# A recurrence and an FFN on one core: 66 elementwise instructions go from VectorE's queue to GpSimd's

## The chip, the core and the metric

The kernel runs as one program on one core of a Trainium2 chip. The metric is the device time of one execution in microseconds (us); the median of three runs stands for a kernel. A core has five engines with a queue of instructions each: TensorE (PE in the profile; its weight loads are PEld), VectorE (DVE), ScalarE (ACT), GpSimd (POOL) and SyncE (SP), which issues the DMAs here. Each engine takes its own instructions strictly in the order of the program; between engines only semaphores order things.

## The reference, cut to what matters

```python
# for each batch and head, over chunks of 32 steps, state is 16 x 32
L = exp(cum[:, None] - cum[None, :]) * causal           # decay inside a chunk
y = ((C @ B.T) * L) @ x  +  (C @ state) * exp(cum)      # within, and from the state
state = exp(sum(la)) * state + sum_j(B_j x_j decay_from_j)
# then all heads side by side make 256 values per token, 3072 tokens
h = x @ w_in                  # 256 -> 2048
out = softplus(h) @ w_out     # 2048 -> 256
```

## The kernel before

**Units.** The 4 x 768 tokens are cut into 24 units of 128 tokens (6 per batch). A unit's work is: `rm`, the table of decays inside the chunk (GpSimd cuts it out of `fc` with an affine select, function `decays`); `bp`, the scaled B (`scale_b`, VectorE); `sp`, the scores (TensorE); `m = sp * rm` (`weigh`, VectorE), which is the last reader of `rm`, whose buffer is then free for the unit two later; `zp`, the product of `bp` and x that updates the state (`update_some`, TensorE, for two units at a time: `zp18` is for units 18 and 19); `yp`, the unit's output (TensorE); and `yy = yp * gg` (`grow_pair`, VectorE).

**Two-part numbers.** The FFN multiplies in a format that keeps too few bits, so each operand is held as a high part and a low part (`xh` and `xl`, `wih` and `wil`, `gh` and `gl`, `woh` and `wol`) and a product is three matmuls: high by high, high by low, low by high. ScalarE makes a high part with a cast, and the low part is what is left (value minus high part). The low part of x is `xl`, two stretches of 256 tokens to a tile of 512; from unit 8 on (tile 2) it is made in the third stage of `grow_pair`.

**Tiles.** The FFN has 6 tiles of 512 tokens. For tiles 0 to 3 it goes plainly: `hp` (first product, 16 blocks `k`), ScalarE's softplus `e`, its parts `gh` and `gl`, and `acc` (second product). Tiles 4 and 5 are done together in eight rounds `p`, by a scheme that needs seven products in place of eight (`seven`), into `late_a` to `late_d`. It takes sums and differences of blocks of weights, made per round in `sums_of_weights`: first `both_w` (one instruction of 512 columns), four instructions `sums_w` of 128 columns, ScalarE's cast into `sw` (high), and one subtract of 512 columns into `sw` (low). Round `p`'s `late_b` is the first product that reads its `sw`. Round 0's sums are made among the units 20 to 23; those of round p + 1 are called, a stage at a time, during round p.

**The order.** Nothing is left to a scheduler: every instruction is marked to keep the program's order, and that order is written out by hand as a text of words, one word for one step (`Y14` is a stage of `grow_pair(14)`, `M16` of `weigh(16)`, `d18` is `decays(18)`, `B18` is `scale_b(18)`, `N18` is `update_some(18)`, `F3.0` is the first product of tile 3, block 0, `sw0` a stage of the sums of round 0). A piece of it, from the place that matters most below:

```python
P2.12 Y14 P2.11 P2.12 Y12 v18 N16 Z2.8 P2.11 v19 d18 F2.13 P2.13 S16 d19 gg18 M16 P2.13 S17 M17 Y14 Z2.9 M16
M17 F2.15 F2.14 B19 B18 v20 P2.12 P2.14 Q19 P2.14 Q18 P2.14 Z2.10 v21 Z2.11 P2.15 N18 N18 F3.0 P2.13 P2.15 C17
```

Buffers matter in one way: the tiles `both_w`, `sums_w`, `again` and `b_rows` take turns in two buffers (tag `w`), and six buffers hold the units' inputs `un`. `V` and `Pl` are VectorE and GpSimd, `A` is ScalarE; `WHOLE` is 12.

Of the kernel before, what the change touches and what calls it, by code (L numbers as in the profile page):

```python
# [10 lines left out]
F32 = mybir.dt.float32  # L11
# [6 lines left out]
ALU = mybir.AluOpType  # L18
PSUM = bass.MemoryType.PSUM

P = 128
# [11 lines left out]
WHOLE = 12  # L33
# [90 lines left out]
def recurrence_then_ffn(ctx: ExitStack, tc: tile.TileContext, un, late, at, al, w_in, w_out, const, outT):  # L124
# [24 lines left out]
    V, A, Pl, PE = (InOrder(e) for e in (nc.vector, nc.scalar, nc.gpsimd, nc.tensor))  # L149
# [12 lines left out]
    wih = cp.tile([P, 2, DFF], F32R, name="wih")  # L162
    wil = cp.tile([P, 2, DFF], F32R, name="wil")
# [247 lines left out]
    def x_parts(t0):  # L411
        j = max(i for i in range(len(sizes)) if starts[i] <= t0)
        if j not in xparts:
            xparts[j] = [p3.tile([P, 2, 512], F32R, tag=f"x{v}", name=f"x{v}_{j}", bufs=3) for v in "hl"]
        return xparts[j], t0 - starts[j]
# [24 lines left out]
    def scale_b(i):  # L440
        b, u = divmod(i, NU)
        if u < NU - 1:
            bp = mid[i]["bp"] = p2.tile([P, NH, N], F32, tag="bp", name=f"bp{i}", bufs=4)
            V.tensor_tensor(
                bp,
                un_s[i][:, U_B:U_C].rearrange("p (h n) -> p h n", n=N),
                f_tok[b][0][:, u, :].unsqueeze(2).broadcast_to([P, NH, N]),
                op=ALU.mult,
            )
# [184 lines left out]
    def grow_pair(i):  # L634
        y = p2.tile([P, 2, 2 * P], F32, tag="yy", name=f"yy{i}")
        if i >= 4 * (PAIRED + 1):
            ys[i % 4 * P] = y
        for g in range(2):
            V.tensor_tensor(y[:, g], mid[i]["yp"][g], gg_s[i, 2][:, g], op=ALU.mult)
        yield  # L640
        (xh, xl), c0 = x_parts(i * P)
        hi = xh[:, :, c0 : c0 + 2 * P]
        A.copy(hi, y)
        yield
        V.tensor_tensor(xl[:, :, c0 : c0 + 2 * P], y, hi.bitcast(F32), op=ALU.subtract)

    def update_some(i):
        some = [v for v in range(2) if i + v < NB * NU and (i + v) % NU < NU - 1]
# [179 lines left out]
    def sums_of_weights(p):  # L828

        def apart_of(w):  # L830
            return w.bitcast(F32).rearrange("p c (h k f) -> p c h k f", h=2, f=P)[:, :, :, p]

        t = p2.tile([P, 2, 2, P], F32, tag="w", name=f"both_w{p}")
        s = p2.tile([P, 4, P], F32, tag="w", name=f"sums_w{p}")
        both = sums_w[p] = p3.tile([P, 2, 4, P], F32R, tag="wraw", name=f"sw{p}", bufs=WRAW)
        V.tensor_tensor(t, apart_of(wih), apart_of(wil), op=ALU.add)
        yield
        V.tensor_tensor(s[:, 0], t[:, 0, 1], t[:, 1, 1], op=ALU.add)
        V.tensor_tensor(s[:, 1], s[:, 0], t[:, 0, 0], op=ALU.subtract)
        yield  # L840
        V.tensor_tensor(s[:, 2], t[:, 0, 0], t[:, 0, 1], op=ALU.subtract)
        V.tensor_tensor(s[:, 3], t[:, 1, 0], s[:, 1], op=ALU.subtract)
        A.copy(both[:, 0], s)
        yield
        V.tensor_tensor(both[:, 1], s, both[:, 0].bitcast(F32), op=ALU.subtract)

    def values_again():
        xh, xl = x_parts(starts[PAIRED])[0]
# [119 lines left out]
    def staged(f):  # L968
# [7 lines left out]
        return step  # L976

    sums_of_weights = staged(sums_of_weights)
    acts = {
        "warm": warm,  # L980
# [21 lines left out]
        "W": staged(split_stages),  # L1002
        "D": staged(lambda i: decays(i, 4 if i < 2 else 2)),
        "B": scale_b,
        "C": scale_c,
        "S": score,
# [13 lines left out]
        "J": within_some,  # L1020
        "N": staged(update_some),
        "Y": staged(grow_pair),
        "L": finish,
        "d": lambda i: whole(decays(i)),
        "Q": split_unit,
        "sw": sums_of_weights,
        "xa": values_again,
        "xs": staged(sums_of_values),
# [28 lines left out]
    for p in range(HALF):  # L1057
# [11 lines left out]
        if p < HALF - 1:  # L1069
            sums_of_weights(p + 1)  # L1070
# [83 lines left out]
```

## Time and profile before

| | |
|---|---|
| three runs | 317.13, 319.83, 319.46 us; median 319.46 us |
| profiled execution, from its first to its last instruction | 315.5 us |
| median less that span | 4.0 us |
| TensorE's granted clock, mean of the span | 0.999 |
| busy: PE, DVE, ACT, POOL | 309.6, 233.4, 194.5, 37.8 us |

The page does not give the time of the profiled execution itself, only its span. The span is what the engines' rows fill, and a run's time is 1.6 to 4.3 us longer than it by the three runs. "Busy" of an engine is the time in which at least one of its instructions runs.

### The profile page before, as it was taken

How to read it: one execution, taken by the hardware profiler on the slowest of the kernel's cores; microseconds unless marked ns; L12 is line 12 of the kernel's file. 1: busy time of each engine (PE TensorE's matmuls, PEld its weight loads, DVE VectorE, ACT ScalarE, POOL GpSimd, SP SyncE). 2: the span in 40 equal slices, each digit the busy share in tenths (PEclk: the TensorE clock that was granted, in tenths of full speed). 3: DMA queues.
4: the chain of work that ended last, by engine and by line, in shares of the span. 5: the costliest groups of instructions: out<-in, count | busy, mean ns of one | idle time of the engine just before them, and what ended most of it. 6: DMA issues, size and time to landing. Idle time of an engine off the chain costs nothing.

```text
span 315.5 us, 5504 instructions
## 1 busy us (share of the span) xinstructions
PE 309.6 (98%) x2081; PEld 246.8 (78%) x2081; DVE 233.4 (74%) x501; ACT 194.5 (62%) x367; POOL 37.8 (12%) x52
## 2 busy tenths in 40 slices
PE   8899999999999999999999999999999999999995
PEld 5557778878778778888887877888888888888884
DVE  4987876957547664789898989948478877877753
ACT  4999977877574244667667445326646567554761
POOL 3452010000003330012303303000000000000000
PEclk9999999999999999999999999999999999999999
DMA  6986075525000430262256022000001000000003
GB/s 209 334 269 229 2 249 179 183 94 163 1 0 3 132 137 0 82 219 66 69 179 208 0 96 92 0 2 1 0 2 66 0 0 2 0 0 2 2 0 133
DMA packets 15323, 26.87 MB, mean 85 GB/s; under 512 B 1472, under 2 KB 6208, under 8 KB 15296
## 3 DMA queue, kind: packets, MB, share of 16 engines
q1 hardware_dynamic: 15296, 26.52, 25.3%
q8 instruction: 16, 0.26, 0.3%
q14 instruction: 11, 0.09, 0.1%
HBM read 22.97 MB, written 3.54 MB: 84 GB/s over the span
## 4 chain that ended last, share of the span: by engine, by line
PE 92%; DMA 3%; SPq 2%; ACT 1%; issue 0%; DVE 0%; DVEq 0%; ACTq 0%
PE hp L146 28%; PE acc L146 28%; PE late_acc L146 13%; PE yp L146 5%; PE late_a L146 4%; PE late_d L146 3%; PE late_c L146 3%; PE sp L146 3%; SPq L155 2%; PE late_b L146 2%; DMA gg<-gd 2%; DMA head_in<-in_un 2%; PE zp L146 1%; PE fp L146 0%; ACT fc L146 0%
## 5 line engine op out<-in xcount | busy, mean ns | idle before, releaser
L146 DVE TENSOR_TENSOR gl<-e,gh 128x512 fp32r<-128x512 f32 x96 | 68.3, 720 | 26.3 <-ACT gh L146 26.2
L146 ACT CAST gh<-e 128x512 fp32r<-128x512 f32 x96 | 59.0, 619 | 25.2 <-PE acc L146 22.3
L146 ACT ACTIVATE e<-hp 128x512 f32<-128x512 f32 x64 | 37.3, 593 | 28.1 <-PE hp L146 28.0
L146 POOL TENSOR_SCALAR_AFFINE_SELECT rm<-fc 128x512 f32<-128x512 f32 (+2 forms) x40 | 34.6, 891 | 154.2 <-DVE m L146 141.4
L146 PE MATMUL hp<-xh,wih 128*128 128x512 f32 (+1 forms) x136 | 52.5, 386 | 0.0
L146 PE MATMUL hp<-xl,wih 128*128 128x512 f32 (+1 forms) x136 | 51.4, 378 | 0.0
L146 PE MATMUL hp<-xh,wil 128*128 128x512 f32 (+1 forms) x136 | 51.2, 377 | 0.0
L146 PE MATMUL acc<-gh,woh 128*128 128x512 f32 x128 | 50.7, 396 | 0.0
L146 PE MATMUL acc<-gl,woh 128*128 128x512 f32 x128 | 49.9, 390 | 0.0
L146 PE MATMUL acc<-gh,wol 128*128 128x512 f32 x128 | 49.9, 389 | 0.0
L146 DVE TENSOR_TENSOR m<-sp,rm 128x256 f32<-128x256 f32 (+1 forms) x80 | 33.7, 467 | 4.5 <-PE sp L146 2.7
L146 ACT ACTIVATE e<-e 128x512 f32<-128x512 f32 x24 | 15.1, 631 | 32.9 <-DVE e L146 32.9
L146 PEld LDWEIGHTS hp<-xh,wih 128*128 128x128 f32 x136 | 25.6, 188 | 6.0 <-issue 0.5
L146 PEld LDWEIGHTS hp<-xh,wil 128*128 128x128 f32 x136 | 25.6, 188 | 4.9
L146 PEld LDWEIGHTS hp<-xl,wih 128*128 128x128 f32 x136 | 25.6, 188 | 4.3
L146 PEld LDWEIGHTS acc<-gh,woh 128*128 128x128 f32 x128 | 24.0, 188 | 6.1 <-issue 1.3
L146 PEld LDWEIGHTS acc<-gh,wol 128*128 128x128 f32 x128 | 24.0, 188 | 5.1
L146 PEld LDWEIGHTS acc<-gl,woh 128*128 128x128 f32 x128 | 24.1, 188 | 4.6
L146 PE MATMUL late_acc<-gh,woh 128*128 128x512 f32 x62 | 24.1, 389 | 0.0
L146 PE MATMUL late_acc<-gl,woh 128*128 128x512 f32 x62 | 24.1, 389 | 0.0
L146 PE MATMUL late_acc<-gh,wol 128*128 128x512 f32 x62 | 24.1, 389 | 0.0
L146 DVE TENSOR_TENSOR yy<-yp,gg 128x256 f32<-128x256 f32 x16 | 6.0, 418 | 12.1 <-PE yp L146 12.1
(154 smaller groups left out, 480.7 us busy)
## 6 DMA issues: line engine op xcount, KB each, us to landing
wraw<-in_w_in SPq DMA_DIRECT2D x8, 512.0 KB, 4.7
wraw<-in_w_out SPq DMA_DIRECT2D x8, 512.0 KB, 3.6
ub<-in_late SPq DMA_DIRECT2D x8, 512.0 KB, 4.2
un<-in_un SPq DMA_DIRECT2D x12, 320.0 KB, 4.4
gg<-gd SPq DMA_DIRECT2D x18, 128.0 KB, 3.7
un<-in_late SPq DMA_DIRECT2D x8, 256.0 KB, 4.4
out_t<-o SPq DMA_DIRECT2D x8, 256.0 KB, 2.1
head_in<-in_un SPq DMA_DIRECT2D x4, 192.0 KB, 4.9
```

The source lines that it names most:

```text
L146: return lambda *a, **k: tc.keep_in_program_order(f(*a, **k))
L155: tc.keep_in_program_order(nc.sync.dma_start(out, in_))
```

## The change

GpSimd in place of VectorE issues three kinds of instruction, each at the same place of the written order: `bp` from unit 12 on (10 instructions, for units 17 and 23 have none), `xl` from tile 2 on (8), and of `sums_of_weights` all but ScalarE's cast (6 in each of 8 rounds).

```diff
@@ scale_b
-            V.tensor_tensor(
+            (V if i < WHOLE else Pl).tensor_tensor(
                 bp,
                 un_s[i][:, U_B:U_C].rearrange("p (h n) -> p h n", n=N),
                 f_tok[b][0][:, u, :].unsqueeze(2).broadcast_to([P, NH, N]),
@@ grow_pair
         A.copy(hi, y)
         yield
-        V.tensor_tensor(xl[:, :, c0 : c0 + 2 * P], y, hi.bitcast(F32), op=ALU.subtract)
+        Pl.tensor_tensor(xl[:, :, c0 : c0 + 2 * P], y, hi.bitcast(F32), op=ALU.subtract)
@@ sums_of_weights
-        V.tensor_tensor(t, apart_of(wih), apart_of(wil), op=ALU.add)
-        yield
-        V.tensor_tensor(s[:, 0], t[:, 0, 1], t[:, 1, 1], op=ALU.add)
-        V.tensor_tensor(s[:, 1], s[:, 0], t[:, 0, 0], op=ALU.subtract)
-        yield
-        V.tensor_tensor(s[:, 2], t[:, 0, 0], t[:, 0, 1], op=ALU.subtract)
-        V.tensor_tensor(s[:, 3], t[:, 1, 0], s[:, 1], op=ALU.subtract)
+        Pl.tensor_tensor(t, apart_of(wih), apart_of(wil), op=ALU.add)
+        yield
+        Pl.tensor_tensor(s[:, 0], t[:, 0, 1], t[:, 1, 1], op=ALU.add)
+        Pl.tensor_tensor(s[:, 1], s[:, 0], t[:, 0, 0], op=ALU.subtract)
+        yield
+        Pl.tensor_tensor(s[:, 2], t[:, 0, 0], t[:, 0, 1], op=ALU.subtract)
+        Pl.tensor_tensor(s[:, 3], t[:, 1, 0], s[:, 1], op=ALU.subtract)
         A.copy(both[:, 0], s)
         yield
-        V.tensor_tensor(both[:, 1], s, both[:, 0].bitcast(F32), op=ALU.subtract)
+        Pl.tensor_tensor(both[:, 1], s, both[:, 0].bitcast(F32), op=ALU.subtract)
```

TensorE's and ScalarE's queues keep their order. VectorE's and GpSimd's change at three places that count. GpSimd's queue around units 16 to 19; the numbers behind the names are the unit (or tile) and a running number:

```order
 L146 AFFINE_SELECT rm16_1957<-fc2_221 128x1024
+L146 TENSOR_TENSOR xl_3_2032<-yy12_1993,xh_3_2031 128x2x256
 L146 AFFINE_SELECT rm18_2056<-fc2_221 128x1024
 L146 AFFINE_SELECT rm19_2073<-fc2_221 128x1024
+L146 TENSOR_TENSOR xl_3_2032<-yy14_2008,xh_3_2031 128x2x256
+L146 TENSOR_TENSOR bp19_2113<-un19_2054,ft2_222 128x128
+L146 TENSOR_TENSOR bp18_2115<-un18_2042,ft2_222 128x128
 L146 AFFINE_SELECT rm20_2249<-fc2_221 128x1024
```

`bp18`, which `zp18` reads, is now the last of five instructions in a row on GpSimd. The same place in VectorE's queue (`x2` is two rows alike):

```order
 L146 TENSOR_TENSOR m_2078<-sp_0_2067,rm_1957 128x512
 L146 TENSOR_TENSOR m_2088<-sp_0_2082,rm_1906 128x512
-L146 TENSOR_TENSOR xl_2032<-yy_2008,xh_2031 128x2x256
 L146 TENSOR_TENSOR m_2078<-sp_1_2068,rm_1957 128x512
 L146 TENSOR_TENSOR m_2088<-sp_1_2083,rm_1906 128x512
-L146 TENSOR_TENSOR bp_2113<-un_2054,ft_222 128x128
-L146 TENSOR_TENSOR bp_2115<-un_2042,ft_222 128x128
 L146 TENSOR_TENSOR gl_2119<-e_2034,gh_2039 128x512
```

The products `m` of units 16 and 17 come sooner, and `gl` follows on them directly. GpSimd's queue at the sums of round 1, after the last `rm` of the program:

```order
 L146 AFFINE_SELECT rm22_2452<-fc2_221 128x1024
+L146 TENSOR_TENSOR xl_5_2664<-yy20_2637,xh_5_2663 128x2x256
+L146 TENSOR_TENSOR xl_5_2664<-yy22_2679,xh_5_2663 128x2x256
+L146 TENSOR_TENSOR both_w1_2815<-wih_78,wil_79 128x512
+L146 TENSOR_TENSOR sums_w1_2816<-both_w1_2815 128x128
+L146 TENSOR_TENSOR sums_w1_2816<-sums_w1_2816,both_w1_2815 128x128
+L146 TENSOR_TENSOR sums_w1_2816<-both_w1_2815 128x128
+L146 TENSOR_TENSOR sums_w1_2816<-both_w1_2815,sums_w1_2816 128x128
+L146 TENSOR_TENSOR sw1_2817<-sums_w1_2816,sw1_2817 128x512
+L146 TENSOR_TENSOR both_w2_2902<-wih_78,wil_79 128x512
```

No work of VectorE stands before these any more: each begins when its inputs, its buffer and GpSimd are there.

## Rows read from the trace of the kernel before

**Rows 1.** The page's first part: busy us (share of span), instructions.

```profile
PE 309.6 (98%) x2081; PEld 246.8 (78%) x2081; DVE 233.4 (74%) x501; ACT 194.5 (62%) x367; POOL 37.8 (12%) x52
```

**Rows 2.** Busy us by stretch: PE, PEld, DVE, ACT, POOL; clock, DMA share, GB/s.

```profile
160.00:180.00 20.00, 20.00 (x110) 16.54 (x109) 18.52 (x37) 12.01 (x21) 4.52 (x4) 1.00 0.47 152
240.00:260.00 20.00, 20.00 (x90) 16.57 (x89) 16.50 (x32) 11.58 (x20) 0.00 (x0) 1.00 0.00 0
```

**Rows 3.** Waits of TensorE: for whom, us in total, times, longest.

```profile
PE yp L146 <- DVE y L146: 0.7, 2, 0.4
```

**Rows 4.** VectorE's groups by form: busy us, mean ns of one, idle before.

```profile
L146 DVE TENSOR_TENSOR xl<-yy,xh 128x512 fp32r<-128x512 f32 x8 | 6.6, 819 | 1.4 <-ACT xh L146 1.4
...
L146 DVE TENSOR_TENSOR sw<-sums_w,sw 128x512 fp32r<-128x512 f32 x8 | 5.5, 691 | 2.4 <-ACT sw L146 2.4
...
L146 DVE TENSOR_TENSOR both_w<-wih,wil 128x512 f32<-128x512 f32 x8 | 5.5, 682 | 0.0
...
L146 DVE TENSOR_TENSOR sums_w<-both_w 128x128 f32<-128x128 f32 x16 | 4.5, 282 | 0.0
```

**Rows 5.** All of GpSimd's affine selects: ns min/median/max, first and last start, forms.

```profile
L146 POOL TENSOR_SCALAR_AFFINE_SELECT rm<-fc x40: 449/727/1720, 6.1 to 195.3; 128x512 f32<-128x512 f32 x20, 128x1024 f32<-128x1024 f32 x12, 128x256 f32<-128x256 f32 x8
```

**Rows 6.** GpSimd's timeline, 107 to 160 us: start, us, instruction, idle before.

```profile
140.97 1.28 POOL L146 TENSOR_SCALAR_AFFINE_SELECT rm<-fc 128x1024 f32<-128x1024 f32 x1 [27.33 <-DVE m L146]
145.30 1.41 POOL L146 TENSOR_SCALAR_AFFINE_SELECT rm<-fc 128x1024 f32<-128x1024 f32 x1 [3.05 <-DVE m L146]
```

**Rows 7.** VectorE's timeline, 144 to 148 us.

```profile
145.48 1.75 DVE L146 TENSOR_TENSOR gl<-e,gh 128x512 fp32r<-128x512 f32 x1
...
147.29 0.68 DVE L146 TENSOR_TENSOR gl<-e,gh 128x512 fp32r<-128x512 f32 x1
```

**Rows 8.** VectorE's timeline, 165 to 171 us.

```profile
165.11 0.68 DVE L146 TENSOR_TENSOR xl<-yy,xh 128x512 fp32r<-128x512 f32 x1
165.71 1.28 DVE L146 TENSOR_TENSOR m<-sp,rm 128x512 f32<-128x512 f32 x2
168.24 1.13 DVE L146 TENSOR_TENSOR bp<-un,ft 128x128 f32<-128x128 f32 x2 [1.25 <-DMA un<-in_late]
...
169.90 1.52 DVE L146 SCALAR_TENSOR_TENSOR c_rows<-ub,kb,c_rows 64x512 fp32r<-64x512 f32 x2
```

**Rows 9.** GpSimd's timeline, 166 to 176 us (units 18 and 19).

```profile
166.53 2.52 POOL L146 TENSOR_SCALAR_AFFINE_SELECT rm<-fc 128x1024 f32<-128x1024 f32 x2 [10.83 <-DVE m L146]
```

**Rows 10.** ScalarE's timeline, 167 to 172 us.

```profile
168.26 1.46 ACT L146 ACTIVATE c_rows<-ub,kb 64x512 fp32r<-64x512 f32 x2
```

**Rows 11.** TensorE's timeline, 167 to 176 us.

```profile
170.38 0.43 PE L146 MATMUL zp<-un,bp 128*32 128x64 f32 x16
```

**Rows 12.** ScalarE's timeline, 233 to 238 us (round 1's `sw`).

```profile
235.05 0.61 ACT L146 CAST sw<-sums_w 128x512 fp32r<-128x512 f32 x1
```

**Rows 13.** VectorE's timeline, 233 to 238 us.

```profile
234.03 0.69 DVE L146 TENSOR_TENSOR gl<-e,gh 128x512 fp32r<-128x512 f32 x1 [0.42 <-ACT gh L146]
234.70 0.69 DVE L146 TENSOR_TENSOR e<-late_c,u 128x512 f32<-128x512 f32 x1
235.70 0.69 DVE L146 TENSOR_TENSOR sw<-sums_w,sw 128x512 fp32r<-128x512 f32 x1 [0.30 <-ACT sw L146]
```

**Rows 14.** TensorE's timeline, 235 to 238 us: use of a `gl`, third matmul of `late_b`.

```profile
236.09 0.39 PE L146 MATMUL late_acc<-gl,woh 128*128 128x512 f32 x1
...
237.00 0.39 PE L146 MATMUL late_b<-sxih,sw 128*128 128x512 f32 x1
```

**Rows 15.** ScalarE's timeline, 117 to 120 us (tile 2's second `xh`).

```profile
117.80 0.62 ACT L146 CAST xh<-yy 128x512 fp32r<-128x512 f32 x1 [1.09 <-DVE yy L146]
```

**Rows 16.** TensorE's timeline, 117 to 121 us: first use of tile 2's `xl`.

```profile
120.20 0.39 PE L146 MATMUL hp<-xl,wih 128*128 128x512 f32 x1
```

**Rows 17.** VectorE's timeline, 215 to 226 us (tile 3's last `gl`).

```profile
223.17 2.05 DVE L146 TENSOR_TENSOR gl<-e,gh 128x512 fp32r<-128x512 f32 x3 [1.53 <-ACT gh L146]
```

**Rows 18.** TensorE's timeline, 221 to 228 us: use of the second of those `gl`.

```profile
225.89 0.39 PE L146 MATMUL acc<-gl,woh 128*128 128x512 f32 x1
```

## The prediction

> **What bounds the kernel now.** I read the page's busy shares first: TensorE is busy in 309.6 of 315.5 us, VectorE in 233.4, GpSimd in 37.8 [rows 1]. An average can hide a stage, so the busy time by stretch comes next: from 40 to 300 us every stretch of 20 us has TensorE busy for all of it, at granted clock 1.00, even where VectorE has 18.52 of 20 us [rows 2]. The list of TensorE's waits says the same from the other side: for VectorE it stood still 0.7 us in two waits [rows 3], both before 40 us, which the change does not touch. TensorE's queue is the bound through the whole stretch of the change, about 107 to 300 us. Time taken off VectorE is therefore worth next to nothing by itself; I give it at most 0.3 us. What can move the end is a moved result that now comes after TensorE wants it, and since TensorE has no idle time in which to catch up, each such lateness goes into the end in full. So the work is to find, for each moved instruction, how long its result lay ready before its first use, and what GpSimd needs for it.
>
> **What is moved.** VectorE loses 66 instructions: 8 xl, 8 both_w, 8 sw, 32 sums_w, 10 bp. By the mean durations [rows 4] the first three come to 8 x (0.819 + 0.682 + 0.691) = 17.5 us and the sums to 32 x 0.282 = 9.0, so with ten bp of some 0.28 about 29 us of 233 go.
>
> **What GpSimd needs for one.** The trace has no two-input instruction on GpSimd, so the price is bounded. Its one-input affine selects take 0.449 us at 256 columns and 0.727 at 512 [rows 5] and 1.28 at 1,024 [rows 6] where nothing disturbs them: about 0.17 us and 1.09 ns for each number read in a lane. The lower end is that a second input costs nothing: 0.73 us for 512 columns, 0.31 for 128. If each input must be read in turn, a two-input instruction of 512 columns reads 1,024 numbers and takes 1.28 us, and one of 128 columns reads 256 and takes 0.45. For the upper end I take the longest select of the trace, 1.72 us [rows 5], and 0.6 for 128 columns in proportion. I take the middle one, for it is nearest to what the instruction does: 24 x 1.28 + 42 x 0.45 = 50 us more on GpSimd, 88 us in all, far from a full engine. The Trainium skill (GPSIMD Engine Reference, section 3.1) gives 4,497 ns for a two-input add of 2,048 columns, so a quarter of that, 1.12 us, would be an estimate for 512; with it the sum below comes to 0.7 us, not 1.2. No run here shows it.
>
> **The port.** VectorE's gl reads two tiles of SBUF, as all moved instructions do. When one began 0.18 us after a GpSimd select, it took 1.75 us and not 0.68, and ended 0.52 us after the select did [rows 6, 7]: it stood until GpSimd let go and then ran its columns. The select behind such a gl in turn grew, up to 1.72 us. So the two engines take turns, and one instruction at a time is the price of a turn. The Trainium skill (Perfetto Trace Analysis, section Optimizing Scalar/DVE Operations) warns that moving work between these two engines might not help because they share a read port. The rows agree; if there were no such turns, the sum below would be about 0.1 us in place of 1.2.
>
> **Place 1: bp18, worth 0.9 us.** Before, VectorE made bp19 and bp18 from 168.24 (when unit 19's input had landed) to 169.38 [rows 8], and zp18 began at 170.38 [rows 11], 1.0 us later, with no idle time on TensorE. After, five instructions stand in a row on GpSimd: rm18, rm19, xl, bp19, bp18. The first may start when m16 is done, 166.40 by the rows [rows 8, 9]; two xl that stood ahead of it on VectorE are gone, 0.60 us of the queue each (165.11 to 165.71 for the second), so it starts 1.2 sooner, at 165.3, and ends at 166.6. VectorE's gl, now directly behind the products, waits for the port until 166.6 and holds it to 167.1; rm19 then ends at 168.3, xl at 169.6. c_rows, which has two SBUF inputs too, gets its first half from ScalarE at 169.0 [rows 10], so it takes the next turn, to 170.1; bp19 runs to 170.4, the second c_rows to 170.95, bp18 to 171.25. With 0.05 us for the semaphore zp18 starts at 171.3 in place of 170.38: **0.9 us lost**. At the low price xl ends at 169.0 and bp18 by 170.2: nothing lost. At the high one xl ends at 170.0 and bp18 at 172.0: 1.7 lost. Tile 3's xl is read only after zp18 and made before bp18. The states that read zp18 move with TensorE and cost nothing more.
>
> **Place 2: sw of round 1, worth 0.3 us.** ScalarE's cast ends at 235.67 [rows 12] and stays there, since it stands behind work that TensorE times, not behind the sums. Before, VectorE's subtract followed at 235.70 to 236.39 [rows 13], and the third matmul of late_b reads it at 237.00 [rows 14]. After, VectorE has its gl at 235.40, right behind e, and holds the port to 236.1; GpSimd's subtract can read from then and ends 1.28 after about 235.95, at 237.2. TensorE is **0.3 us late** (none at the low price, 0.7 at the high). In round 2 the distance from cast to use is already longer by about half a microsecond, and from round 3 on by more; there it is hidden at every price taken here.
>
> **Places that cost nothing at the middle price.** Tile 2's second xl: the cast ends at 118.42 [rows 15], a gl may hold the port to 118.97, the subtract ends at 120.1, its use is at 120.20 [rows 16]; at the high price 0.4 lost. The selects rm12 and rm13, which ran at 111 us, now stand behind bp14 and so run by 132 at the latest; their products come at 139.6, so 7 us cover them. bp12 to bp16 and bp20 to bp22 have over 2 us to their zp. Round 0's sums end about 1 us later than on VectorE, ScalarE's cast behind them too, and ScalarE idles longer than that a little later. In each of the last eight rounds GpSimd holds the port for 2 x 1.28 + 4 x 0.45 = 4.4 us, yet VectorE has 0.68 + 0.69 + 4 x 0.28 = 2.5 us less to do there, and a gl is delayed by one turn, 1.28 at most; the tightest, in the first round, ends at 234.72 [rows 13] and is used at 236.09 [rows 14], 1.37 later. The DMAs that refill un now wait for bp on GpSimd, done long before.
>
> **Sum.** 0.9 + 0.3 = 1.2 us on a span of 315.5, so 316.7; the median of the runs lies 4.0 above the span, and 319.46 + 1.2 = 320.7 us.
>
> **Rivals.** *Nothing is lost.* GpSimd is as quick as at the low price, or the turns fall well: 319.5 us, perhaps 319.2. For it: the margins missed are short. Against it: a second input would have to be free. *Slower: the price is high and the lateness spreads.* The mechanism is GpSimd's chain ahead of the last rounds. From 217 us xl, both_w and four sums take turns with VectorE's sums of x, every one with two SBUF inputs; at 1.28 that chain ends about 1 us later than before and tile 3's second last-stage gl, which has 1.43 us (224.46 to 225.89) [rows 17, 18], is just in time. At 1.72 it is 0.9 us late. With 1.7 at bp18, 0.7 at sw, 0.4 at tile 2 and 0.3 at the scores of unit 17, whose b_rows wait a turn longer behind xl, that makes 4.0: 323.5 us, and beyond it bp22, held behind round 0's sums, adds over 1 us: 325. It passes 1% (3.2 us) from a price of about 1.6 us for 512 columns. *Faster.* VectorE's 29 us would have to shorten TensorE's queue; with TensorE at 20.00 of 20 us [rows 2] there is nothing for it to shorten but gaps too short to be listed: 318.9 at best by the profile, below 316.3 only if the profile hides a stall.
>
> **How the numbers follow.** The three runs of one kernel spread over 2.7 us, so 1% is about what a measurement here can tell from no change. I give the forecast (320 to 322.4) 0.55, nothing lost 0.17, the spreading lateness 0.24, faster by over 1% 0.04. Within 1% is 0.72. The range goes from nothing lost on a lucky set of runs, 317.6, to the high price with its first spreading, 324.5.
>
> **What would show it.** In the changed kernel's profile the two-input instructions on GpSimd should take near 1.28 us at 512 columns and 0.45 at 128 when undisturbed. TensorE's waits should have a new row for GpSimd's bp, near 0.9 us and once, at zp18, and one for sw, near 0.3, at round 1. The steps before 107 us should lie as before. The prediction is wrong if a two-input instruction takes over 1.6 us, if the selects rm become what VectorE's m waits for, or if TensorE waits for gl in the last rounds.

## The result, and the profile after

The changed kernel takes 320.03 us (median of 20 runs, 318.94 to 325.37); the kernel before, with 20 runs, the three shown above among them, 317.33 us (316.04 to 320.23). The ratio is 1.0079, 95% interval 1.0053 to 1.0105: about 2.5 us more. It leaves out two slow runs of the changed kernel, 324.13 and 325.37 us. The prediction was 1.2 us more, on a median of three runs, 319.46, that lies 2.1 us above that of the twenty. The page's first part, for [rows 1], in a profiled execution with a span of 317.5 us:

```profile
PE 311.0 (98%) x2081; PEld 247.3 (78%) x2081; DVE 224.8 (71%) x435; ACT 194.0 (61%) x367; POOL 96.5 (30%) x118
```

VectorE lost 66 instructions, 29 us by their mean durations, and its busy time fell by only 8.6 us. GpSimd gained 58.7. The stretches of [rows 2] and the list of TensorE's waits, for [rows 3]:

```profile
160.00:180.00 20.00, 18.49 (x103) 15.12 (x102) 17.43 (x30) 11.05 (x19) 8.13 (x7) 1.00 0.47 152
240.00:260.00 20.00, 20.00 (x90) 16.56 (x89) 14.24 (x20) 12.62 (x22) 11.54 (x14) 1.00 0.06 24
```

```profile
PE warm L146 <- POOL some L146: 1.0, 1, 1.0
PE zp L146 <- POOL bp L146: 0.9, 1, 0.9
PE sp L146 <- DVE b_rows L146: 0.6, 1, 0.6
PE yp L146 <- DVE y L146: 0.3, 1, 0.3
```

TensorE now stands still for 1.5 of the 20 us from 160 us on, at granted clock 1.00 as before; where the sums run (240 to 260 us) it is as full as it was. Two waits are new: zp for GpSimd's bp, which the prediction asked for, and sp, the scores, for VectorE's `b_rows`, an instruction that the change does not touch. The row for sw that it asked for as well is not in the list. (`warm` and `yp` lie ahead of the first moved instruction.)

The list leaves out short gaps, and the head of the program, which the change does not touch, differs from one execution to the next: at 108.5 us the eleven other traces of this document lie from 1.2 us ahead of the kernel before to 1.5 us behind it. So I set each of TensorE's 2,081 matmuls beside the same matmul of the trace before and took the difference of the starts. From 108.5 us (just ahead of the first moved instruction) to the end this lateness grows by **2.41 us**, in single steps:

| step (time in the trace before) | lateness added, us | predicted at the middle price |
|---|---|---|
| tile 2's first use of xl (120.20) | 0.07 | 0 |
| scores of unit 17 (162.98) | **0.82** | 0 |
| zp18 (170.38) | 1.01 | 0.9 |
| tile 3's last gl at acc (225.89) | 0.14 | 0, just in time |
| round 1's sw at late_b (237.00) | 0.37 | 0.3 |

At 108.5 us the changed kernel was 0.43 us ahead; 2.41 - 0.43 = 1.98 us is the difference of the two spans. The table is the ledger that the experiments below are read by: it needs no median, so it tells a few tenths apart where a ratio of this kernel cannot. It rests on one trace of each kernel; where a place is left alone its step comes again (0.8 us at unit 17 also in e1, e6 and e8, 0.3 to 0.4 at round 1 also in e3 and e6 to e10).

**The step that nobody had in the sum.** VectorE's timeline of the kernel before, at unit 17, 159 to 164 us, then the same place of the changed one on VectorE, GpSimd and TensorE:

```profile
160.30 1.52 DVE L146 SCALAR_TENSOR_TENSOR c_rows<-ub,kb,c_rows 64x512 fp32r<-64x512 f32 x2
161.85 0.75 DVE L146 SCALAR_TENSOR_TENSOR b_rows<-ub,kb,b_rows 128x512 fp32r<-128x512 f32 x1
```

```profile
159.97 2.48 DVE L146 SCALAR_TENSOR_TENSOR c_rows<-ub,kb,c_rows 64x512 fp32r<-64x512 f32 x2
162.48 0.75 DVE L146 SCALAR_TENSOR_TENSOR b_rows<-ub,kb,b_rows 128x512 fp32r<-128x512 f32 x1
```

```profile
159.82 1.30 POOL L146 TENSOR_TENSOR xl<-yy,xh 128x512 fp32r<-128x512 f32 x1 [4.26 <-ACT xh L146]
```

```profile
163.38 0.71 PE L146 MATMUL sp<-c_rows,b_rows 128*128 128x256 f32 x4 [0.57 <-DVE b_rows L146]
```

Tile 3's first xl starts on GpSimd 0.15 us ahead of `c_rows`, which has two inputs in SBUF as well. The first of the two `c_rows` is held until GpSimd is done (at 161.12) and ends half a microsecond after it, so the pair takes 2.48 us and not 1.52. Before, `b_rows` ended at 162.60 and the scores of unit 17 began at 162.98. Of these 0.38 us, 0.15 is what the scores need behind `b_rows` even when they wait for it (163.23 to 163.38 in the changed kernel), so 0.23 us were there to cover a loss of 0.96 us; the other 0.73 is TensorE's step at the first of these matmuls, and the next ones add the rest of the 0.82.

**Place 1, bp18,** on GpSimd, VectorE and TensorE, for [rows 8, 9, 11]:

```profile
165.96 2.95 POOL L146 TENSOR_SCALAR_AFFINE_SELECT rm<-fc 128x1024 f32<-128x1024 f32 x2 [4.84 <-DVE m L146]
168.88 1.29 POOL L146 TENSOR_TENSOR xl<-yy,xh 128x512 fp32r<-128x512 f32 x1
170.14 1.66 POOL L146 TENSOR_TENSOR bp<-un,ft 128x128 f32<-128x128 f32 x2
```

```profile
166.34 1.43 DVE L146 TENSOR_TENSOR gl<-e,gh 128x512 fp32r<-128x512 f32 x1
...
169.47 2.06 DVE L146 SCALAR_TENSOR_TENSOR c_rows<-ub,kb,c_rows 64x512 fp32r<-64x512 f32 x2 [1.70 <-ACT c_rows L146]
```

```profile
171.85 0.43 PE L146 MATMUL zp<-un,bp 128*32 128x64 f32 x16 [0.94 <-POOL bp L146]
```

The five instructions stand in a row without a gap. The turns with VectorE's gl and `c_rows` show in the two selects (2.95 us, 2.52 in [rows 9]) and in the two bp (1.66 us, 0.76 undisturbed in e6 below), and zp18 begins 0.05 us after the last. **Place 2,** round 1's sw, on GpSimd and TensorE, for [rows 13, 14]:

```profile
237.38 1.41 POOL L146 TENSOR_TENSOR sw<-sums_w,sw 128x512 fp32r<-128x512 f32 x1 [10.59 <-ACT sw L146]
```

```profile
238.84 0.50 PE L146 MATMUL late_b<-sxih,sw 128*128 128x512 f32 x1
```

GpSimd had waited 10.59 us for ScalarE's cast, so no queue stands ahead of this subtract: it is late by its own length.

**Prices,** by GpSimd's groups (busy us, mean ns of one, idle before):

```profile
L146 POOL TENSOR_TENSOR both_w<-wih,wil 128x512 f32<-128x512 f32 x8 | 13.4, 1672 | 0.0
L146 POOL TENSOR_TENSOR sw<-sums_w,sw 128x512 fp32r<-128x512 f32 x8 | 11.1, 1384 | 38.8 <-ACT sw L146 38.8
L146 POOL TENSOR_TENSOR xl<-yy,xh 128x512 fp32r<-128x512 f32 x8 | 10.7, 1343 | 34.2 <-ACT xh L146 34.2
L146 POOL TENSOR_TENSOR sums_w<-both_w 128x128 f32<-128x128 f32 x16 | 9.5, 595 | 3.1 <-DVE sxol L146 2.6
```

The shortest xl takes 1.28 us, the shortest sums_w 0.46, the shortest bp, of 128 columns too, 0.40; the means are longer by the turns. VectorE's own groups paid for part of the relief; gl in the kernel before, and after:

```profile
L146 DVE TENSOR_TENSOR gl<-e,gh 128x512 fp32r<-128x512 f32 x96 | 68.3, 720 | 26.3 <-ACT gh L146 26.2
```

```profile
L146 DVE TENSOR_TENSOR gl<-e,gh 128x512 fp32r<-128x512 f32 x96 | 78.4, 827 | 33.1 <-ACT gh L146 32.3
```

The 96 gl alone grew by 10.1 us, `c_rows` by 1.5 (its mean went from 745 to 840 ns).

### The profile page after: what moved, and what is told of

It reads as the page before. It is cut to its first block, busy times and chain, and to the rows that moved or that the text cites. A ratio compares the mean times of both kernels' runs of the same rounds, so it can differ in the third digit from the quotient of the medians.

```text
span 317.5 us, 5527 instructions
## 1 busy us (share of the span) xinstructions
PE 311.0 (98%) x2081; PEld 247.3 (78%) x2081; DVE 224.8 (71%) x435; ACT 194.0 (61%) x367; POOL 96.5 (30%) x118
## 4 chain that ended last, share of the span: by engine, by line
PE 88%; ACT 3%; DMA 3%; DVE 2%; POOL 1%; SPq 1%; issue 1%; DVEq 0%; POOLq 0%
PE hp L146 27%; PE acc L146 26%; PE late_acc L146 13%; PE yp L146 5%; PE sp L146 3%; PE late_a L146 3%; PE late_d L146 3%; PE late_c L146 3%; PE late_b L146 2%; DMA gg<-gd 2%; PE warm L146 1%; DMA gd<-lr 1%; DVE c_rows L146 1%; PE zp L146 1%; SPq L155 1%
## 5 line engine op out<-in xcount | busy, mean ns | idle before, releaser
L146 DVE TENSOR_TENSOR gl<-e,gh 128x512 fp32r<-128x512 f32 x96 | 78.4, 827 | 33.1 <-ACT gh L146 32.3
L146 POOL TENSOR_TENSOR sw<-sums_w,sw 128x512 fp32r<-128x512 f32 x8 | 11.1, 1384 | 38.8 <-ACT sw L146 38.8
```

What stands on the lines that cost most here:

```text
L146: return lambda *a, **k: tc.keep_in_program_order(f(*a, **k))
```

## The experiments

Theory A: the lateness arises at a few single places, each from GpSimd's queue or from a turn at the port just there. Rival B: it is spread, in proportion to the time that GpSimd works beside VectorE. In each experiment "lateness" is the growth from 108.5 us to the end, as in the table above.

### One kind at a time: e1, e2, e3

Three kernels that make one part of the change alone.

```diff
e1:  - V.tensor_tensor(xl[...], y, hi, ...)      + Pl.tensor_tensor(...)
e2:  - V.tensor_tensor(bp, ...)                  + (V if i < WHOLE else Pl).tensor_tensor(bp, ...)
e3:  - V.tensor_tensor(t / s[:, k] / both[:, 1]) + Pl.tensor_tensor(...)
```

> Only the 8 low parts of x go to GpSimd; bp and the sums of weights stay on VectorE. Theory A (three places: TensorE is late only where one moved result, or one turn at the port, comes after its first use): TensorE is late once at the scores of unit 17, by 0.8 us, because VectorE's c_rows of unit 17 waits one turn of 1.3 us behind the low part of tile 3; at tile 2's first use 0.1; at zp18 0 to 0.2, since bp18 stays on VectorE but may wait a turn. Sum 0.9 to 1.1 us over before. Theory B (spread: the loss is in proportion to the time that GpSimd holds the port): xl is 10.7 of the 60 us of moved instructions, so 0.4 us of the 2.4, and no wait of its own at unit 17.

Measured: ratio 1.0045 (1.0005 to 1.0085); lateness 1.37 us, of it 0.36 at tile 2, **0.78 at the scores of unit 17**, 0.23 at those of unit 18. VectorE and GpSimd, 160 to 166 us:

```profile
161.42 2.47 DVE L146 SCALAR_TENSOR_TENSOR c_rows<-ub,kb,c_rows 64x512 fp32r<-64x512 f32 x2
```

```profile
161.27 1.30 POOL L146 TENSOR_TENSOR xl<-yy,xh 128x512 fp32r<-128x512 f32 x1 [4.43 <-ACT xh L146]
```

The pair of the changed kernel, with the same 0.15 us between the starts. The unit 17 step belongs to xl alone. That at unit 18 comes from bp19 on VectorE, which starts 0.3 us later against TensorE than before: when its input lands, after 2.55 us of waiting.

> Only the 10 scaled B from unit 12 on go to GpSimd. Theory A: TensorE is late once, at zp18, by 0.7 to 1.0 us: without the low part in the queue bp19 and bp18 come one instruction of 1.3 us sooner, but the two low parts that stay on VectorE let rm18 start 0.6 to 1.2 us later, and each bp still waits a turn behind c_rows (0.85 us, not 0.40). Sum 0.7 to 1.0. Theory B: bp is 7.0 of 60 us, so 0.3 us. A theory without turns at the port (GpSimd only slower by itself): rm19 ends at 169.0, bp18 at 169.9, zp18 is not late at all, 0.

Measured: ratio 1.0015 (0.9979 to 1.0052), not to be told from no change; lateness 0.69, all of it at zp18 (0.74 there). GpSimd, 166 to 173 us:

```profile
166.72 2.95 POOL L146 TENSOR_SCALAR_AFFINE_SELECT rm<-fc 128x1024 f32<-128x1024 f32 x2 [10.63 <-DVE m L146]
169.64 1.62 POOL L146 TENSOR_TENSOR bp<-un,ft 128x128 f32<-128x128 f32 x2
```

With xl still ahead of m on VectorE the selects start later, and no xl stands among them; the two nearly cancel (0.74 against 1.01). The theory without turns at the port, by which nothing is lost here, fails.

> Only the sums of weights (48 instructions, 42 of the 60 us on GpSimd) go to GpSimd. Theory A: TensorE is late at the low part of round 1's sw, by 0.3 to 0.4 us, and by 0.1 at tile 3's last gl; nothing in rounds 2 to 7. Sum 0.3 to 0.5. Theory B: 70 per cent of 2.4, so 1.7 us.

Measured: ratio 1.0047 (1.001 to 1.0084); lateness 1.33, of it 0.36 at round 1 as in the change, and **0.91 at zp20**, a place that the change does not have. VectorE in the kernel before, then VectorE and GpSimd here, 181 to 187 us:

```profile
179.41 2.35 DVE L146 TENSOR_TENSOR gl<-e,gh 128x512 fp32r<-128x512 f32 x2
```

```profile
180.87 3.43 DVE L146 TENSOR_TENSOR gl<-e,gh 128x512 fp32r<-128x512 f32 x2
184.23 1.27 DVE L146 TENSOR_TENSOR parts_c<-un,kb 128x256 f32<-128x256 f32 x2
185.43 1.00 DVE L146 TENSOR_TENSOR bp<-un,ft 128x128 f32<-128x128 f32 x2
```

```profile
182.07 1.69 POOL L146 TENSOR_TENSOR both_w<-wih,wil 128x512 f32<-128x512 f32 x1
183.83 0.79 POOL L146 TENSOR_TENSOR sums_w<-both_w 128x128 f32<-128x128 f32 x1
```

Round 0's sums run right behind GpSimd's two selects for units 20 and 21, take turns with the second gl, both `parts_c` and both bp of VectorE, and so hold up zp20. In the change bp20, bp21 and two xl stand on GpSimd ahead of these sums, which start at 189.99 us there. The three parts add up to 3.39 us; less the 0.91 that only e3 has, 2.48, against 2.41 for the whole. That this comes so close is luck, for place by place parts and whole differ: 0.36 and 0.07 at tile 2, 0.23 and nothing at unit 18, 0.74 and 1.01 at zp18, nothing and 0.14 at tile 3's last gl. A held for the kind of loss, single places, but its sums for e1 (0.9 to 1.1) and e3 (0.3 to 0.5) were too small: a part alone is late where the whole is not. B fares badly: GpSimd works 10.8, 6.3 and 41.3 us more in e1, e2 and e3 than in the kernel before, and the lateness is 1.37, 0.69 and 1.33 us, in no proportion to it.

### Four instructions back: e4

```diff
- (V if i < WHOLE else Pl)    + (V if i < WHOLE or i in (18, 19) else Pl)   # bp
- Pl (xl)                     + (V if i == 12 else Pl)
- Pl (last subtract into sw)  + (V if p == 1 else Pl)
```

> The change, with four of its 66 instructions back on VectorE: bp18, bp19, the first low part of tile 3, and the low part of round 1's sw. Theory A: all three places are mended, 0 to 0.3 us over before. Theory B: 62 of 66 instructions still on GpSimd, about 2.2 us over before.

Measured: ratio 1.0042 (1.0005 to 1.008); lateness 1.09. The steps at unit 17, zp18 and round 1 are gone, 2.2 us with four of 66 instructions. But 0.68 came up at the scores of unit 18. VectorE and GpSimd, 166 to 177 us:

```profile
168.39 1.38 DVE L146 TENSOR_TENSOR bp<-un,ft 128x128 f32<-128x128 f32 x2 [2.28 <-DMA un<-in_late]
...
175.59 0.28 DVE L146 SCALAR_TENSOR_TENSOR state<-state,fr,zp 128x64 f32<-128x64 f32 x1
```

```profile
168.13 1.29 POOL L146 TENSOR_TENSOR xl<-yy,xh 128x512 fp32r<-128x512 f32 x1
```

The two bp, back on VectorE, end 0.7 us later against TensorE than before, and so does what follows them on VectorE (`c_rows`, `b_rows` and the state of unit 19); TensorE's wait for that state is 0.4 us. About 0.25 of the 0.7 is a turn behind GpSimd's xl (the pair takes 1.38 us, 1.13 in [rows 8]). The rest comes ahead of it: bp19 starts when unit 19's input lands, after 2.28 us of waiting, and in this execution that was 0.4 us later against TensorE than before. Whether the step at unit 18 belongs to this kernel or to this execution is open. A's sum, 0 to 0.3, was too small here as well.

### Only where nothing is short: e5

GpSimd keeps 49 of the 66: xl from unit 16 on, bp from unit 20 on, the sums of all rounds but 1.

```diff
- (V if i < WHOLE else Pl)   + (V if i < APART else Pl)    # bp; APART is 20
- Pl (xl)                    + (V if i < 16 else Pl)
- Pl (sums of round p)       + (V if p == 1 else Pl)
```

> On GpSimd stay only the low parts of x from unit 16 on, the scaled B from unit 20 on and the sums of weights of all rounds but round 1; all of units 12 to 19 and round 1 is back on VectorE (52 of 66... 48 of the moved instructions are 4 low parts, 3 bp and 42 of the sums, 49 in all, still on GpSimd). Theory A (queue place and turns at five known places): every known place is mended, TensorE is late by 0 to 0.2 us in all from 108.5 us on, and the median is within 0.2 per cent of before. Theory B (spread by time on GpSimd): some 75 per cent of 2.4, so 1.8 us.

Measured: ratio 0.999 (0.9955 to 1.0024), lateness **0.02 us**. The page's first part and all of TensorE's listed waits:

```profile
PE 309.8 (99%) x2081; PEld 247.3 (79%) x2081; DVE 226.3 (72%) x452; ACT 194.0 (62%) x367; POOL 81.3 (26%) x101
```

```profile
PE warm L146 <- POOL some L146: 1.0, 1, 1.0
```

43.5 us more on GpSimd than before, 7.1 less on VectorE, and nothing lost or won. That refutes B, and relief of VectorE is worth nothing in this ledger.

### Place 1 by its order and its length: e6, e8

e6 puts the two bp ahead of the second xl in GpSimd's row; e8 issues that xl twice.

```diff
e6:  - ... S17 M17 Y14 Z2.9 M16        + ... S17 M17 Z2.9 M16
     - M17 F2.15 F2.14 B19 B18 v20     + M17 F2.15 F2.14 B19 B18 Y14 v20
e8:  + if i == 14: Pl.tensor_tensor(xl[...], y, hi, ...)   # the same subtract, a first time
```

> The change, with one word of the written order moved: the second low part of tile 3 stands behind bp19 and bp18 in GpSimd's queue, not ahead of them. If zp18's 1.0 us is the place in the queue: bp18 comes 1.3 us sooner, zp18 is not late, and the low part, now behind, is 0 to 0.6 us late for tile 3's first product; sum of both 0 to 0.6 in place of 1.0. If it is GpSimd's speed at bp itself, zp18 stays 0.5 to 1.0 late. The other places as in the change: 0.8 at the scores of unit 17, 0.4 at round 1, 0.1 to 0.2 at tile 3's last gl.

Measured (one run, 318.33 us): lateness 1.61; the step at zp18 is gone, that at unit 17 stays at 0.82, and tile 3's first use of xl is 0.10 late. GpSimd, 164 to 176 us, and TensorE:

```profile
168.88 0.76 POOL L146 TENSOR_TENSOR bp<-un,ft 128x128 f32<-128x128 f32 x2
169.60 1.74 POOL L146 TENSOR_TENSOR xl<-yy,xh 128x512 fp32r<-128x512 f32 x1
```

```profile
170.68 0.43 PE L146 MATMUL zp<-un,bp 128*32 128x64 f32 x16
...
171.39 0.50 PE L146 MATMUL hp<-xl,wih 128*128 128x512 f32 x1
```

> The change, with the second low part of tile 3 issued twice on GpSimd, one after the other (the same result). If lateness at zp18 goes into the end in full: one more instruction of 1.29 us ahead of bp19 and bp18, with or without one more turn of c_rows (0.53), so zp18 2.3 to 2.9 us late in place of 1.0, and the end 1.3 to 1.9 us later than with the change. If TensorE has slack further on that takes lateness up: the step at zp18 grows as much, but the end less.

Measured (one run, 321.08 us): zp18 is 2.70 us late in place of 1.01, the lateness at the end 4.16 in place of 2.41. GpSimd, and TensorE's wait:

```profile
169.01 2.97 POOL L146 TENSOR_TENSOR xl<-yy,xh 128x512 fp32r<-128x512 f32 x2
171.94 1.66 POOL L146 TENSOR_TENSOR bp<-un,ft 128x128 f32<-128x128 f32 x2
```

```profile
PE zp L146 <- POOL bp L146: 2.6, 1, 2.6
```

The second xl takes 1.68 us more, zp18 comes 1.69 later and the end 1.75: at this place a microsecond more on GpSimd was a microsecond more of the kernel.

### Unit 17: a busy GpSimd, or one that reads? e7, e9, e10

All three replace tile 3's first xl on GpSimd. e7 and e9 leave out the low part of these 256 tokens (zeros), e10 puts the high part in its place.

```diff
e7:   + if i == 12: 3 x Pl.memset(xl[...], 0.0)
e9:   + if i == 12: Pl.memset(xl[...], 0.0); 3 x Pl.memset(y, 0.0)   # y is read by the cast
e10:  + if i == 12: Pl.tensor_copy(xl[...], hi)
```

> The change, but the first low part of tile 3 is not computed: three memsets of the same 512 columns stand in its place, so the low part of 256 tokens is zero there. GpSimd is busy as long (about 1.3 us) from the same moment, but reads nothing. If the turn at the read port is the cause at unit 17, c_rows beside it takes 0.73 us, not 1.69, and the 0.8 us at the scores of unit 17 are gone. If it is anything else of GpSimd's being busy (a write port, a semaphore), c_rows still waits for the memsets and 0.3 to 0.8 us stay. zp18 and round 1 as in the change, 1.0 and 0.4.

Measured (one run, 319.42 us): lateness 1.48, no step at unit 17. But it tells less than it was meant to: the memsets had no cast to wait for and ran from 156.71 to 158.40 us, over before unit 17's `c_rows` began (161.14). e9 repeats it with memsets that wait for the cast.

> The change, but the first low part of tile 3 is not computed (zero there, set early); at its place GpSimd waits for the same cast of ScalarE and then sets the tile yy, which nobody reads any more, to zero three times, some 1.7 us that write and read nothing beside VectorE's c_rows of unit 17. If the read side of the port is what c_rows waits for: c_rows takes 0.73 to 0.75 us, and no step at the scores of unit 17. If any work of GpSimd holds VectorE up: c_rows takes 1.2 to 1.7 us and a step of 0.3 to 0.8 us stays.

Measured (one run, 318.01 us): lateness 1.41, no step at unit 17. GpSimd and VectorE:

```profile
159.55 1.70 POOL L146 MEMSET yy<- 128x512 f32 x3 [3.74 <-ACT xh L146]
```

```profile
159.73 1.52 DVE L146 SCALAR_TENSOR_TENSOR c_rows<-ub,kb,c_rows 64x512 fp32r<-64x512 f32 x2
```

GpSimd is busy for 1.70 us at the very place, longer than with xl, and the two `c_rows` take 1.52 us as before the change. Place 1 shrank with it: zp18 is 0.78 us late, not 1.01 (e7: 0.77). TensorE's wait and GpSimd's selects:

```profile
PE zp L146 <- POOL bp L146: 0.7, 1, 0.7
```

```profile
164.69 2.96 POOL L146 TENSOR_SCALAR_AFFINE_SELECT rm<-fc 128x1024 f32<-128x1024 f32 x2 [3.44 <-DVE m L146]
```

Set beside the kernel before, by each trace's lateness at that place, rm18 starts at 164.69 + 0.58 = 165.27 us here and at 165.96 - 0.46 = 165.50 in the change: VectorE's m16, which it waits for, is done that much sooner.

> The change, but the first low part of tile 3 is replaced by a copy of the high part on GpSimd, which waits for the same cast and reads one tile of 512 columns, not two. If c_rows waits for whatever reads on GpSimd: the copy takes some 0.73 us, so c_rows is held about 0.55 us and takes 1.1 to 1.2 us, and the step at the scores of unit 17 falls from 0.8 to some 0.2 to 0.3 us. If only a two-input instruction holds it up: c_rows takes 0.73 us and there is no step.

Measured (one run, 320.51 us): lateness 1.72, a step of 0.12 at unit 17 and 0.99 at zp18. GpSimd and VectorE:

```profile
161.73 0.61 POOL L146 CAST xl<-xh 128x512 fp32r<-128x512 f32 x1 [4.24 <-ACT xh L146]
```

```profile
161.90 1.76 DVE L146 SCALAR_TENSOR_TENSOR c_rows<-ub,kb,c_rows 64x512 fp32r<-64x512 f32 x2
```

One input, half the numbers, holds `c_rows` for 0.24 us (1.76 against 1.52, less than expected), two inputs for 0.96. At this place it is GpSimd's reading that VectorE waits for, and until the instruction is done: in the change as here the first `c_rows` ends 0.54 us after it. The Trainium skill (SBUF — State Buffer, section Who interferes with whom) says the same: a VectorE instruction with two SBUF inputs contends with a GpSimd instruction that reads SBUF, not with one that only writes it; e9 and e10 agree.

## Why the prediction was right, and which term it missed

The sign, the bound and the form were right: TensorE stays the bound, lateness goes into the end in full (e8: 1.69 in, 1.75 out), and it comes from a few places (e4 removes 2.2 us with four instructions, e5 keeps 49 at 0.02 us). Within 1% held too: 0.8%. The sum was short: 1.2 predicted, 2.4 in the ledger, and the absolute figure came near by luck (last point).

- **The price of a two-input instruction** was taken as 1.28 us at 512 columns and 0.45 at 128; undisturbed it is 1.28 and 0.46, the middle one to a hundredth, and 0.40 for bp, the instruction of place 1. The prediction's estimate by the Trainium skill (GPSIMD Engine Reference, section 3.1), 1.12, is below it, and the measurement decides. Of the signs of being wrong that it named one came by the letter, a two-input instruction over 1.6 us: both_w, at a mean of 1.67, but with the turns in it, for the shortest takes 1.29 (e3). The others did not come: VectorE's m waits for rm 1.6 us, once, before and after, and TensorE has no listed wait for gl.
- **Place 1, bp18:** 0.9 predicted, 1.01 measured. By the clock of the kernel before and without the two earlier steps (171.85 + 0.43 - 0.89), zp18 begins at 171.4; predicted was 171.3. e6 and e8 show that the row of five, in its order, is the cause. The near hit is in part luck: with nothing to hold VectorE at unit 17, zp18 is 0.78 late (e9), so the row by itself was put 0.1 too high and 0.23 of the 1.01 comes from the term below.
- **Place 2, round 1's sw:** 0.3 predicted, 0.37 measured, 0.36 in e3, none in e4. The later rounds lose nothing, as predicted.
- **The places at zero:** tile 2 lost 0.07 and tile 3's last gl 0.14, each called covered or just in time. Together 0.2 us.
- **The scores of unit 17: the term that failed.** The prediction named them only in the rival with the high price, at 0.3 us, and put them at nothing at the middle price. They lost 0.82 at the middle price. It had asked, for each moved instruction, how long its result lay ready before its first use; xl's result is in time here. What is late is VectorE's `c_rows` and `b_rows`, which were not moved: the moved xl starts 0.15 us ahead of them and reads for 1.3 us (e1 has the step with xl alone, e4 loses it with that one xl back, e9 when GpSimd only writes). The prediction's own section on the port held the rule; it was applied at place 1, where a result was late, and not to VectorE's chain at unit 17, whose cover was at most 0.38 us by the trace of before. With the 0.23 at place 1 it is worth 1.05 of the 2.41 us.
- **The rivals.** Lost nothing: wrong, but e5 shows that it was to be had with 49 of the instructions. Spreading lateness at a high price: the price was not high and nothing spread; its term at unit 17 was the one right thing in it. Faster: no; e5 takes 7.1 us off VectorE at a ratio of 0.999.
- **The absolute figure.** With 0.82 and the two small ones the sum would have been 0.9 + 0.3 + 0.8 + 0.2 = 2.2 us. 320.7 came near 320.03 by luck: the median of three runs before was 2.1 us too high, and the added loss about as much as 1.5 us too low (320.03 - 317.33 = 2.7). Nor is a run 4.0 us longer than its profiled span: every run on record is 1.7 to 1.8 us longer than its own span (319.25 and 317.5 us here), and the rest of the 4.0 is that the median belonged to another, longer execution.

Open: the steps of e5 are nil at every kept place in one execution, but its interval reaches from 0.45% faster to 0.24% slower. The single-run kernels (e6 to e10) were read by the ledger alone. No version here beats the kernel before.

## What to carry to other kernels

Where one engine is full, as here, work moved between two others had nothing to win, and it lost at the few places with little cover, where a result lies ready only just before it is wanted: list them from the trace before moving anything, and leave those instructions where they are. Ask of each moved instruction two things, when its own result is wanted, and which instruction of the other engine that also reads two tiles of SBUF begins while it runs, with what that chain has to spare. An engine's relief is not the sum of what it gave away: here 29 us went and 8.6 us of busy time did.

## What the hardware showed that was not expected

- A memset on GpSimd beside a VectorE instruction with two SBUF inputs costs the latter nothing (1.52 us for two, e9); a one-input read of 512 columns costs 0.24 us (e10), a two-input one 0.96 (the change). At this place it was GpSimd's reads, not its busy time, that VectorE felt.
- A second input cost GpSimd what as many more columns did: 1.28 us for a subtract of two inputs of 512 columns, 1.28 for a select of one of 1,024 [rows 6]. For bp, whose second input repeats one number over 16 columns, it cost less: 0.40 us and not 0.46.
- Turns hit both sides at once: e3's first both_w took 1.69 us in place of 1.28, and the two gl there 3.43 in place of 2.35 (the first of them stands behind a select in both kernels), where an undisturbed gl takes 0.68 [rows 7].
